# Sliding-window attention followed by spectral mixing: heads taken in pairs, deeper rings, and the on-chip accumulator banks dealt out anew

## The chip, the cores and the metric

The kernel runs on one core of a Trainium2 chip. The core has five engines that work side by side and wait for each other through semaphores: TensorE (PE in the profile, with its weight loads as PEld), VectorE (DVE), ScalarE (ACT), GpSimd (POOL) and SyncE (SP). Sixteen DMA engines move data between the main memory and the on-chip memory (SBUF). Matmul results land in a small accumulator memory (PSUM) of eight banks, from which ACT and DVE read them. The metric is the device time of one execution in microseconds (us), lower is better.

The kernel is written against a layer that takes tiles from pools, puts in every semaphore by itself, and lays out the order of each engine's instructions at compile time. A pool with `bufs=n` has n buffers for each kind of tile; a tile waits for its buffer until the last reader of the earlier tile is done. An operation written `nc.any` may be given to ACT, DVE or (a memset) POOL by that layer. So an edit in the source can move instructions that it doesn't name.

## The reference

The inputs are `q`, `k`, `v` of shape 8 x 8 x 576 x 64 (batch, heads, positions, head dimension), the mixing weights `moe_w_r` and `moe_w_i` of shape 64 x 512 x 512 (one matrix for each of 64 modes) and `moe_w_ch`, 512 x 512. All are float32, and so is the output, 8 x 576 x 512.

```python
def _attn_ref(q, k, v):
    window = 64
    scores = 1.0 / np.sqrt(D) * np.matmul(q, k.transpose(0, 1, 3, 2))
    rel = pos[:, None] - pos[None, :]
    mask = (rel >= 0) & (rel < window)
    scores = np.where(mask, scores, -1000000000.0)
    scores = scores - np.max(scores, axis=-1, keepdims=True)
    attn = np.exp(scores)
    attn = attn / (np.sum(attn, axis=-1, keepdims=True) + 1e-09)
    return np.matmul(attn, v)

def _moe_ref(x, w_r, w_i, w_ch):
    X = np.fft.rfft(x, axis=1)
    Xr, Xi = (np.real(X[:, :n_modes]), np.imag(X[:, :n_modes]))
    Yr = np.einsum('bmd,mde->bme', Xr, w_r) - np.einsum('bmd,mde->bme', Xi, w_i)
    Yi = np.einsum('bmd,mde->bme', Xr, w_i) + np.einsum('bmd,mde->bme', Xi, w_r)
    Y[:, :n_modes] = Yr + 1j * Yi
    y = np.fft.irfft(Y, n=S, axis=1)
    u = x + y
    return u + np.maximum(u @ w_ch, 0.0)
```

The second function takes the first one's output, with the heads laid side by side to 512 columns. A position attends only to itself and to the 63 positions before it.

## The kernel before

There are three stages.

**Attention and forward transform.** For each batch (8) and pair of heads (4), `build_qT` loads q and k as bf16 through POOL's queue, with two heads side by side in the 128 columns, and turns them with TensorE, so that the first head lies in partitions 0 to 63 and the second in 64 to 127. For each head, `stage_a` computes, for each block of 128 keys, the scores of those keys against up to 256 queries (a contraction over 64 rows), takes the exponential on ACT and multiplies by a 0/1 mask on DVE. `stage_b` multiplies the result with v, which carries a column of ones so that the sum of the weights comes out as column 65, and divides on DVE. After the eighth head of a batch, `dft_batch` takes the first 64 modes of the transform over the positions.

```python
    with ExitStack() as p1:
        qkraw = p1.enter_context(tc.tile_pool(name="qkraw", bufs=4))
        qtpool = p1.enter_context(tc.tile_pool(name="qtpool", bufs=3))
        vpool = p1.enter_context(tc.tile_pool(name="vpool", bufs=4))
        etpool = p1.enter_context(tc.tile_pool(name="etpool", bufs=12))
        smallpool = p1.enter_context(tc.tile_pool(name="smallpool", bufs=12))
        # ... (cut: xstg; the PSUM pools are ps_tr 2, ps_tr64 1, ps_s 2, ps_o 2, ps_d 1)

        def build_qT(src5, b, hp, name):
            # ... (cut: qT, ptr and raw are taken; two loads of 512 positions, one a head, on POOL's queue)
            for c in range(4):
                raw2 = raw[:, c, :, :].rearrange("p h d -> p (h d)")
                nc.tensor.transpose(out=ptr[:, c * 128:(c + 1) * 128], in_=raw2,
                                    identity=ident_bf[:, :])
            # ... (cut: a load of the last 64 positions into rawt, seen as raw3)
            ptr2 = ps_tr64.tile([128, 64], QT_DTYPE, name="pstr64")
            nc.tensor.transpose(out=ptr2[:, :64], in_=raw3, identity=ident_bf[:64, :64])
            nc.any.tensor_copy(out=qT[:, 512:576], in_=ptr2[:, :64])
            nc.any.tensor_copy(out=qT[:, 0:512], in_=ptr[:, 0:512])
            return qT

        def load_v(b, h):
            # ... (cut: vs, fp32, two loads on SP's queue; its column of ones by nc.any.memset)
            vt = vpool.tile([128, NKB, D + 1], ET_DTYPE, name="vt")
            nc.any.tensor_copy(out=vt[:, 0:4, :], in_=vs[:, 0:4, :])
            nc.any.tensor_copy(out=vt[0:64, 4, :], in_=vs[0:64, 4, :])
            return vt

        def stage_a(b, h, pp, qT, kT):
            ets = []
            for c in range(NKB):
                # ... (cut: nk, q0, nq: 128 x 256 three times, 128 x 192, 64 x 64)
                pss = ps_s.tile([128, ETW], FP32, name="pss")
                nc.tensor.matmul(out=pss[:nk, :nq], lhsT=kT[pp, q0:q0 + nk],
                                 rhs=qT[pp, q0:q0 + nq], start=True, stop=True)
                et = etpool.tile([128, ETW], ET_DTYPE, name="et")
                nc.scalar.activation(out=et[:nk, :nq], in_=pss[:nk, :nq],
                                     func=ACT_F.Exp, scale=EX_SCALE)
                nc.vector.tensor_tensor(out=et[:nk, :nq], in0=et[:nk, :nq],
                                        in1=m01[:nk, :nq], op=ALU.mult)
                ets.append((et, nk, nq))
            return ets

        def stage_b(b, h, ets, vt):
            for qb in range(NKB):
                # ... (cut: nq2, and the tiles of this block and of the one before)
                pso = ps_o.tile([128, D + 1], FP32, name="pso")
                nc.tensor.matmul(out=pso[:nq2, :], lhsT=et_c[:nk_c, 0:nq2],
                                 rhs=vt[:nk_c, qb, :], start=True, stop=(qb == 0))
                if qb >= 1:
                    nc.tensor.matmul(out=pso[:nq2, :], lhsT=et_p[:nk_p, 128:128 + nq2],
                                     rhs=vt[:nk_p, qb - 1, :], start=False, stop=True)
                rcp = smallpool.tile([128, 1], FP32, name="rcp")
                nc.vector.reciprocal(out=rcp[:nq2, :], in_=pso[:nq2, D:D + 1])
                nc.vector.tensor_scalar(out=x_sb[:nq2, b, qb, h * 64:h * 64 + 64],
                                        in0=pso[:nq2, 0:D], scalar1=rcp[:nq2, :],
                                        scalar2=None, op0=ALU.mult)
        # ... (cut: dft_batch: five matmuls into psX, a copy Xs, four transposes psXT, copies into XQ)
```

The loop runs head by head and keeps one head pending: `stage_a` of a head is written ahead of `stage_b` of the head before it.

**Mixing.** For each of 64 modes two weight matrices of 512 KB (as bf16 on chip) are loaded through POOL's queue into a pool of 22 buffers, which is filled while attention runs. Sixteen rows (8 batches, real and imaginary) are multiplied with them.

```python
        for m in range(NM):
            wr = wtpool.tile([128, NDCH, DM], W_DTYPE, name="wr", tag="wt")
            wi = wtpool.tile([128, NDCH, DM], W_DTYPE, name="wi", tag="wt")
            nc.gpsimd.dma_start(out=wr, in_=moe_w_r[m].rearrange("(c p) e -> p c e", p=128))
            nc.gpsimd.dma_start(out=wi, in_=moe_w_i[m].rearrange("(c p) e -> p c e", p=128))
            # ... (cut: eight matmuls into psm, a copy stg, a store into Yall)
```

**Inverse transform and channel product.** For each batch and block of positions: two matmuls into `psy`, the sum `ut` with attention's output, four transposes `psut`, four matmuls `pout` with `moe_w_ch`, and the output `ot`.

Of the kernel before, what the change touches and what calls it, by code (L numbers as in the profile page):

```python
# [10 lines left out]
FP32 = mybir.dt.float32  # L11
# [3 lines left out]
ALU = mybir.AluOpType  # L15
ACT_F = mybir.ActivationFunctionType

WINDOW = 64
# [3 lines left out]
QT_DTYPE = BF16  # L22
ET_DTYPE = BF16
Y_DTYPE = BF16
DEBUG_OUT = "full"
DEBUG_HL = (0, 1)
# [3 lines left out]
def kernel(  # L30
# [10 lines left out]
    nc = tc.nc  # L41
    B, H, S, D = q.shape
# [4 lines left out]
    EX_SCALE = 1.0 / float(np.sqrt(D))  # L47

    HP = H // 2
# [13 lines left out]
    nc.gpsimd.memset(m01f, 1.0)  # L63
    nc.gpsimd.affine_select(
        out=m01f, in_=m01f, compare_op=ALU.is_ge, fill=0.0,
        base=0, pattern=[[1, ETW]], channel_multiplier=-1,
    )
    nc.gpsimd.affine_select(
        out=m01f, in_=m01f, compare_op=ALU.is_ge, fill=0.0,
        base=WINDOW - 1, pattern=[[-1, ETW]], channel_multiplier=1,  # L70
    )
    m01 = consts.tile([128, ETW], BF16, name="m01")
    nc.vector.tensor_copy(out=m01, in_=m01f)

    MAGIC = 12582912.0
    PSAFE = 3.14159
# [78 lines left out]
    Yall = ypool.tile([NM, 2, B, DM], Y_DTYPE, name="Yall")  # L155

    with ExitStack() as p1:
        qkraw = p1.enter_context(tc.tile_pool(name="qkraw", bufs=4))
        qtpool = p1.enter_context(tc.tile_pool(name="qtpool", bufs=3))
        vpool = p1.enter_context(tc.tile_pool(name="vpool", bufs=4))  # L160
        etpool = p1.enter_context(tc.tile_pool(name="etpool", bufs=12))
        smallpool = p1.enter_context(tc.tile_pool(name="smallpool", bufs=12))
        xstg = p1.enter_context(tc.tile_pool(name="xstg", bufs=2))
        ps_tr = p1.enter_context(tc.tile_pool(name="ps_tr", bufs=2, space=bass.MemoryType.PSUM))
        ps_tr64 = p1.enter_context(tc.tile_pool(name="ps_tr64", bufs=1, space=bass.MemoryType.PSUM))
        ps_s = p1.enter_context(tc.tile_pool(name="ps_s", bufs=2, space=bass.MemoryType.PSUM))
# [28 lines left out]
        def load_v(b, h):  # L195
            vs = vpool.tile([128, NKB, D + 1], FP32, name="vs")
            nc.sync.dma_start(
                out=vs[:, 0:4, 0:D],
                in_=v[b, h, 0:512, :].rearrange("(c p) d -> p c d", p=128),
            )  # L200
            nc.sync.dma_start(out=vs[0:64, 4:5, 0:D],
                              in_=v[b, h, 512:576, :].rearrange("(c p) d -> p c d", p=64))
            nc.any.memset(vs[:, :, D:D + 1], 1.0)  # L203
            vt = vpool.tile([128, NKB, D + 1], ET_DTYPE, name="vt")
            nc.any.tensor_copy(out=vt[:, 0:4, :], in_=vs[:, 0:4, :])
            nc.any.tensor_copy(out=vt[0:64, 4, :], in_=vs[0:64, 4, :])
            return vt

        def stage_a(b, h, pp, qT, kT):
            ets = []  # L210
            for c in range(NKB):
                nk = min(128, S - c * 128)
                q0 = c * 128
                nq = min(ETW, S - q0)
                pss = ps_s.tile([128, ETW], FP32, name="pss")
                nc.tensor.matmul(out=pss[:nk, :nq],  # L216
                                 lhsT=kT[pp, q0:q0 + nk],
                                 rhs=qT[pp, q0:q0 + nq],
                                 start=True, stop=True)
                et = etpool.tile([128, ETW], ET_DTYPE, name="et")  # L220
                nc.scalar.activation(out=et[:nk, :nq], in_=pss[:nk, :nq],  # L221
                                     func=ACT_F.Exp, scale=EX_SCALE)
                nc.vector.tensor_tensor(out=et[:nk, :nq], in0=et[:nk, :nq],  # L223
                                        in1=m01[:nk, :nq], op=ALU.mult)
                ets.append((et, nk, nq))
            return ets

        def stage_b(b, h, ets, vt):
            for qb in range(NKB):
# [34 lines left out]
                nc.scalar.mul(out=XQ[:, dch, :, b], in_=psXT[:, NM:2 * NM], mul=-1.0)  # L264

        pending = None
        last_of_batch = {}
        nheads = B * H
        for x in range(nheads):
            b, h = divmod(x, H)  # L270
            hp, hl = divmod(h, 2)
            if hl == 0:
                qT = build_qT(q, b, hp, "qTt")
                kT = build_qT(k, b, hp, "kTt")
            pp = slice(hl * 64, hl * 64 + 64)
            if hl in DEBUG_HL:
                vt = load_v(b, h)
                ets = stage_a(b, h, pp, qT, kT)
            if pending is not None:
                stage_b(*pending)  # L280
                pb = pending[0]
                if pending[1] == H - 1 and DEBUG_OUT not in ("x", "qt"):
                    dft_batch(pb)
            pending = (b, h, ets, vt) if hl in DEBUG_HL else None
        if pending is not None:
            stage_b(*pending)
            if DEBUG_OUT not in ("x", "qt"):
                dft_batch(pending[0])

    if DEBUG_OUT in ("x", "qt", "xq"):  # L290
        if DEBUG_OUT == "qt":
# [100 lines left out]
```

The softmax here doesn't subtract the row's maximum and nothing guards it: scores larger than these inputs give would overflow.

## Time and profile before

| what | value |
|---|---|
| time, median of 4 runs | 685.84 us (684.93 to 686.52) |
| span of the profiled execution | 683.9 us, 8003 instructions |
| mean granted TensorE clock | 0.932 |
| PE busy | 497.4 us (73%) in 2200 matmuls |
| PEld busy | 215.9 us (32%) |
| DVE busy | 250.6 us (37%) |
| ACT busy | 246.5 us (36%) |
| POOL busy | 239.8 us (35%) |
| DMA | 98.06 MB, mean 143 GB/s |

The profile comes from the hardware profiler. A line such as `L233 PE MATMUL pso<-vt,et 128*128 128x65 bf16` gives the source line, the engine, the operation, the tile written and the tiles read, and for a matmul the rows and columns of the array in use, then the shape of what streams through. In the kernel before, L181 and L190 are the transposes in `build_qT`, L191 and L192 the copies after them, L205 and L206 the casts to `vt`, L216, L221 and L223 the score, exponential and mask of `stage_a`, L233 and L239 the two matmuls of `stage_b`, L244 and L245 its division, L253 and L260 the transform, L309 and L310 the weight loads. Matmuls overlap each other, and their ends are modelled, so the distance between two starts says more than a duration. The shares of busy time are means over the three stages; each stage has to be read by itself.

### The profile page before, as it was taken

How to read it: one execution, taken by the hardware profiler on the slowest of the kernel's cores; microseconds unless marked ns; L12 is line 12 of the kernel's file. 1: busy time of each engine (PE TensorE's matmuls, PEld its weight loads, DVE VectorE, ACT ScalarE, POOL GpSimd, SP SyncE). 2: the span in 40 equal slices, each digit the busy share in tenths (PEclk: the TensorE clock that was granted, in tenths of full speed). 3: DMA queues.
4: the chain of work that ended last, by engine and by line, in shares of the span. 5: the costliest groups of instructions: out<-in, count | busy, mean ns of one | idle time of the engine just before them, and what ended most of it. 6: DMA issues, size and time to landing. Idle time of an engine off the chain costs nothing.

```text
span 683.9 us, 8003 instructions
## 1 busy us (share of the span) xinstructions
PE 497.4 (73%) x2200; PEld 215.9 (32%) x2200; DVE 250.6 (37%) x1167; ACT 246.5 (36%) x716; POOL 239.8 (35%) x384
## 2 busy tenths in 40 slices
PE   2788998989898988788455465455455455799996
PEld 1443444444444443323111111111111111455553
DVE  5875766666666666800000000000000000456654
ACT  4856666666666666343111111111111111122221
POOL 9885766665545420032223233232232220000000
PEclk9999999999999999999888888888888888899999
DMA  9999999999767641039999999999999999122232
GB/s 117 118 120 168 153 177 157 176 164 149 71 69 72 69 55 27 0 56 209 207 207 207 207 207 207 207 207 208 207 207 207 207 207 151 63 90 103 99 109 92
DMA packets 191165, 98.06 MB, mean 143 GB/s; under 512 B 119440, under 2 KB 186000, under 8 KB 191120
## 3 DMA queue, kind: packets, MB, share of 16 engines
q0 software_dynamic: 144912, 77.62, 82.4%
q1 hardware_dynamic: 46208, 19.94, 11.7%
q8 instruction: 17, 0.28, 0.2%
q14 instruction: 28, 0.23, 0.1%
HBM read 163.58 MB, written 9.44 MB: 253 GB/s over the span
## 4 chain that ended last, share of the span: by engine, by line
DMA 40%; PE 36%; ACT 9%; issue 8%; DVE 6%; SPq 1%; ACTq 0%; POOL 0%; POOLq 0%; DVEq 0%
DMA wi<-in_moe_w_i_dram 39%; PE pss L216 8%; PE pout L352 7%; PE pstr L181 5%; PE pso L233 5%; ACT utt L349 3%; PE psut L345 3%; ACT et L221 3%; PE pso L239 2%; PE psX L253 2%; PE psXT L260 2%; DVE et L223 1%; DVE x_sb L245 1%; PE pstr L190 1%; DVE rcp L244 1%
## 5 line engine op out<-in xcount | busy, mean ns | idle before, releaser
L315 PE MATMUL psm<-wi,XQ 128*16 128x512 bf16 x256 | 120.0, 469 | 100.4 <-DMA wi<-in_moe_w_i_dram 100.3
L313 PE MATMUL psm<-wr,XQ 128*16 128x512 bf16 x256 | 119.6, 467 | 23.5 <-DMA wr<-in_moe_w_r_dram 21.1
L221 ACT ACTIVATE et<-pss 128x256 bf16<-128x256 f32 (+2 forms) x320 | 106.4, 353 | 69.7 <-PE pso L239 37.9
L342 DVE TENSOR_TENSOR ut<-x_sb,psy 128x512 f32<-128x512 bf16 (+1 forms) x40 | 27.2, 685 | 283.9 <-PE psy L336 282.6
L318 ACT CAST stg<-psm 16x512 bf16<-16x512 f32 x63 | 36.2, 575 | 244.8 <-PE psm L315 240.2
L216 PE MATMUL pss<-qT 64*128 64x256 bf16 (+2 forms) x320 | 100.3, 342 | 21.8 <-ACT et L221 17.4
L309 POOL DMA_DIRECT2D wr<-in_moe_w_r_dram x64 | 47.9, 748 | 122.5 <-PE psm L313 60.4
L245 DVE TENSOR_SCALAR x_sb<-pso,rcp 128x64 bf16<-128x64 f32 (+1 forms) x320 | 89.3, 281 | 0.8
L313 PEld LDWEIGHTS <-XQ 128*16 128x16 bf16 x256 | 24.9, 97 | 192.3 <-issue 131.9
L310 POOL DMA_DIRECT2D wi<-in_moe_w_i_dram x64 | 47.9, 749 | 96.5 <-DMA wi<-in_moe_w_i_dram 84.4
L244 DVE RECIPROCAL rcp<-pso 128x1 f32<-128x1 f32 (+1 forms) x320 | 52.6, 164 | 78.0 <-PE pso L239 57.1
L233 PE MATMUL pso<-vt,et 128*128 128x65 bf16 (+1 forms) x320 | 76.3, 244 | 5.2 <-DVE x_sb L245 3.7
L223 DVE TENSOR_TENSOR et<-et,m 128x256 bf16<-128x256 bf16 (+2 forms) x320 | 78.1, 250 | 3.7 <-ACT et L221 3.2
L239 PE MATMUL pso<-vt,et 128*128 128x65 bf16 (+1 forms) x256 | 61.4, 248 | 0.0
L233 PEld LDWEIGHTS <-et 128*128 128x128 bf16 (+1 forms) x320 | 37.5, 118 | 69.3 <-DVE x_sb L245 34.6
L181 PE MATMUL pstr<-ident_bf,raw 128*128 128x128 bf16 x256 | 48.5, 302 | 12.9 <-DVE vs L203 8.3
L175 POOL DMA_DIRECT2D raw<-in_q_dram x64 | 49.1, 773 | 19.7 <-PE pstr L190 11.5
L352 PE MATMUL pout<-wch,utt 128*128 128x512 f32 (+1 forms) x160 | 48.1, 426 | 7.0 <-ACT utt L349 6.4
L175 POOL DMA_DIRECT2D raw<-in_k_dram x64 | 49.5, 785 | 8.7 <-PE pso L233 6.7
L349 ACT CAST utt<-psut 128x512 fp32r<-128x512 f32 (+1 forms) x39 | 21.1, 542 | 76.1 <-PE psut L345 76.1
L216 PEld LDWEIGHTS <-qT 64*128 64x128 bf16 (+1 forms) x320 | 32.1, 106 | 44.2 <-issue 25.2
L359 DVE SCALAR_TENSOR_TENSOR ot<-pout,ut 128x512 f32<-128x512 f32 (+1 forms) x40 | 27.6, 690 | 38.1 <-PE pout L352 38.1
(82 smaller groups left out, 479.1 us busy)
## 6 DMA issues: line engine op xcount, KB each, us to landing
wr<-in_moe_w_r_dram POOLq DMA_DIRECT2D x64, 512.0 KB, 20.0
wi<-in_moe_w_i_dram POOLq DMA_DIRECT2D x64, 512.0 KB, 20.0
vs<-in_v_dram SPq DMA_DIRECT2D x64, 128.0 KB, 3.2
out_dram<-ot SPq DMA_DIRECT2D x32, 256.0 KB, 2.0
raw<-in_q_dram POOLq DMA_DIRECT2D x64, 64.0 KB, 3.1
raw<-in_k_dram POOLq DMA_DIRECT2D x64, 64.0 KB, 3.5
vs<-in_v_dram SPq DMA_DIRECT2D x64, 16.0 KB, 3.1
wch<-in_moe_w_ch_dram POOLq DMA_DIRECT2D x1, 1024.0 KB, 7.5
```

Of the source, the lines that this page charges most:

```text
L175: nc.gpsimd.dma_start(out=raw[:, :, hh, :], in_=src5[b, 2 * hp + hh, 0:512, :].rearrange("(c t) d -> t c d", t=128),)
L181: nc.tensor.transpose(out=ptr[:, c * 128:(c + 1) * 128], in_=raw2, identity=ident_bf[:, :])
L216: nc.tensor.matmul(out=pss[:nk, :nq], lhsT=kT[pp, q0:q0 + nk], rhs=qT[pp, q0:q0 + nq], start=True, stop=True)
L221: nc.scalar.activation(out=et[:nk, :nq], in_=pss[:nk, :nq], func=ACT_F.Exp, scale=EX_SCALE)
L223: nc.vector.tensor_tensor(out=et[:nk, :nq], in0=et[:nk, :nq], in1=m01[:nk, :nq], op=ALU.mult)
L233: nc.tensor.matmul(out=pso[:nq2, :], lhsT=et_c[:nk_c, 0:nq2], rhs=vt[:nk_c, qb, :], start=True, stop=(qb == 0))
L239: nc.tensor.matmul(out=pso[:nq2, :], lhsT=et_p[:nk_p, 128:128 + nq2], rhs=vt[:nk_p, qb - 1, :], start=False, stop=True)
L244: nc.vector.reciprocal(out=rcp[:nq2, :], in_=pso[:nq2, D:D + 1])
L245: nc.vector.tensor_scalar(out=x_sb[:nq2, b, qb, h * 64:h * 64 + 64], in0=pso[:nq2, 0:D], scalar1=rcp[:nq2, :], scalar2=None, op0=ALU.mult)
L313: nc.tensor.matmul(out=psm[:, :], lhsT=XQ[:, dch, m, B:3 * B], rhs=wr[:, dch, :], start=(dch == 0), stop=False)
L315: nc.tensor.matmul(out=psm[:, :], lhsT=XQ[:, dch, m, 0:2 * B], rhs=wi[:, dch, :], start=False, stop=(dch == NDCH - 1))
L352: nc.tensor.matmul(out=pout[:nt, :], lhsT=utt[:, ech * nt:(ech + 1) * nt], rhs=wch[:, ech, :], start=(ech == 0), stop=(ech == NDCH - 1))
```

## The change

The loop goes over pairs of heads. The scores of both heads for one block of keys are written one after the other: first the two matmuls, then the two exponentials and masks. `stage_b` follows for both heads of the pair before. With more tiles in flight, the rings of buffers grow: the `et` ring from 12 to 20, `qkraw` from 4 to 6, `vpool` from 4 to 5, the ring of `rcp` from 12 to 16. The transpose of the last 64 positions goes into the same bank as the other four, which makes one copy of 576 columns out of two (64 and 512) and frees a bank; `ps_o` gets it, 3 instead of 2. The float32 mask is built in a pool that is given back, which frees the room. It is meant to keep more independent work in flight for TensorE and to let the two heads' scores stand side by side. The mixing and the last stage are as they were.

```diff
-    m01f = consts.tile([128, ETW], FP32, name="m01f")
...  (cut: the lines that fill m01f, the same in both)
+    with tc.tile_pool(name="mask_tmp", bufs=1) as mtmp:
+        m01f = mtmp.tile([128, ETW], FP32, name="m01f")

-        qkraw = p1.enter_context(tc.tile_pool(name="qkraw", bufs=4))
+        qkraw = p1.enter_context(tc.tile_pool(name="qkraw", bufs=6))
         qtpool = p1.enter_context(tc.tile_pool(name="qtpool", bufs=3))
-        vpool = p1.enter_context(tc.tile_pool(name="vpool", bufs=4))
-        etpool = p1.enter_context(tc.tile_pool(name="etpool", bufs=12))
-        smallpool = p1.enter_context(tc.tile_pool(name="smallpool", bufs=12))
+        vpool = p1.enter_context(tc.tile_pool(name="vpool", bufs=5))
+        etpool = p1.enter_context(tc.tile_pool(name="etpool", bufs=20))
+        smallpool = p1.enter_context(tc.tile_pool(name="smallpool", bufs=16))
-        ps_tr64 = p1.enter_context(tc.tile_pool(name="ps_tr64", bufs=1, space=bass.MemoryType.PSUM))
         ps_s = p1.enter_context(tc.tile_pool(name="ps_s", bufs=2, space=bass.MemoryType.PSUM))
-        ps_o = p1.enter_context(tc.tile_pool(name="ps_o", bufs=2, space=bass.MemoryType.PSUM))
+        ps_o = p1.enter_context(tc.tile_pool(name="ps_o", bufs=3, space=bass.MemoryType.PSUM))

-            ptr = ps_tr.tile([128, 512], QT_DTYPE, name="pstr")
+            ptr = ps_tr.tile([128, S], QT_DTYPE, name="pstr")
-            ptr2 = ps_tr64.tile([128, 64], QT_DTYPE, name="pstr64")
-            nc.tensor.transpose(out=ptr2[:, :64], in_=raw3, identity=ident_bf[:64, :64])
-            nc.any.tensor_copy(out=qT[:, 512:576], in_=ptr2[:, :64])
-            nc.any.tensor_copy(out=qT[:, 0:512], in_=ptr[:, 0:512])
+            nc.tensor.transpose(out=ptr[:, 512:576], in_=raw3, identity=ident_bf[:64, :64])
+            nc.any.tensor_copy(out=qT[:, :], in_=ptr[:, :])

-        def stage_a(b, h, pp, qT, kT):
...  (cut: its body, shown above)
+        def stage_a_pair(b, hp, qT, kT):
+            ets_pair = ([], [])
             for c in range(NKB):
+                psss = []
+                for hl in range(2):
+                    pp = slice(hl * 64, hl * 64 + 64)
+                    pss = ps_s.tile([128, ETW], FP32, name="pss")
+                    nc.tensor.matmul(out=pss[:nk, :nq],
+                                     lhsT=kT[pp, q0:q0 + nk],
+                                     rhs=qT[pp, q0:q0 + nq],
+                                     start=True, stop=True)
+                    psss.append(pss)
+                for hl in range(2):
+                    et = etpool.tile([128, ETW], ET_DTYPE, name="et")
+                    nc.scalar.activation(out=et[:nk, :nq], in_=psss[hl][:nk, :nq],
+                                         func=ACT_F.Exp, scale=EX_SCALE)
+                    nc.vector.tensor_tensor(out=et[:nk, :nq], in0=et[:nk, :nq],
+                                            in1=m01[:nk, :nq], op=ALU.mult)
+                    ets_pair[hl].append((et, nk, nq))
+            return ets_pair

-        for x in range(nheads):
...  (cut: the loop over heads)
+        for b in range(B):
+            for hp in range(HP):
                 qT = build_qT(q, b, hp, "qTt")
                 kT = build_qT(k, b, hp, "kTt")
+                vts = (load_v(b, 2 * hp), load_v(b, 2 * hp + 1))
+                ets_pair = stage_a_pair(b, hp, qT, kT)
+                if pending is not None:
+                    pb, php, pets, pvts = pending
+                    for hl in range(2):
+                        stage_b(pb, 2 * php + hl, pets[hl], pvts[hl])
+                    if php == HP - 1:
+                        dft_batch(pb)
+                pending = (b, hp, ets_pair, vts)
```

After the loop, the last pair's `stage_b` and the last batch's transform follow in the same way.

More of the change, by code (lines that the diff above doesn't have):

```diff
@@ L60 @@
     nc.vector.tensor_copy(out=ident_bf, in_=ident)
-    m01f = consts.tile([128, ETW], FP32, name="m01f")
[L63 to L71, printed above, removed]
-    m01 = consts.tile([128, ETW], BF16, name="m01")
-    nc.vector.tensor_copy(out=m01, in_=m01f)
+    m01 = consts.tile([128, ETW], BF16, name="m01")
+    with tc.tile_pool(name="mask_tmp", bufs=1) as mtmp:
+        m01f = mtmp.tile([128, ETW], FP32, name="m01f")
+        nc.gpsimd.memset(m01f, 1.0)
+        nc.gpsimd.affine_select(
+            out=m01f, in_=m01f, compare_op=ALU.is_ge, fill=0.0,
+            base=0, pattern=[[1, ETW]], channel_multiplier=-1,
+        )
+        nc.gpsimd.affine_select(
+            out=m01f, in_=m01f, compare_op=ALU.is_ge, fill=0.0,
+            base=WINDOW - 1, pattern=[[-1, ETW]], channel_multiplier=1,
+        )
+        nc.vector.tensor_copy(out=m01, in_=m01f)
     MAGIC = 12582912.0
@@ L207, in load_v @@
             return vt
-        def stage_a(b, h, pp, qT, kT):
-            ets = []
+        def stage_a_pair(b, hp, qT, kT):
+            ets_pair = ([], [])
             for c in range(NKB):
@@ L214, in stage_a @@
                 nq = min(ETW, S - q0)
[L215 to L226, printed above, removed]
+                psss = []
[15 more added lines that the diff above has]
+            return ets_pair
         def stage_b(b, h, ets, vt):
@@ L266 @@
         pending = None
-        last_of_batch = {}
-        nheads = B * H
-        for x in range(nheads):
-            b, h = divmod(x, H)
-            hp, hl = divmod(h, 2)
-            if hl == 0:
+        for b in range(B):
+            for hp in range(HP):
                 qT = build_qT(q, b, hp, "qTt")
                 kT = build_qT(k, b, hp, "kTt")
[L275 to L284, printed above, removed]
+                vts = (load_v(b, 2 * hp), load_v(b, 2 * hp + 1))
[7 more added lines that the diff above has]
+                pending = (b, hp, ets_pair, vts)
         if pending is not None:
-            stage_b(*pending)
-            if DEBUG_OUT not in ("x", "qt"):
-                dft_batch(pending[0])
+            pb, php, pets, pvts = pending
+            for hl in range(2):
+                stage_b(pb, 2 * php + hl, pets[hl], pvts[hl])
+            dft_batch(pb)
     if DEBUG_OUT in ("x", "qt", "xq"):
```

## The prediction

> **What bounds the kernel now.** I read the page's slices first, to cut the run into stages, then the table by stage, then the chain of work that ended last, in order of time, then TensorE's timeline inside one stage, and the waits last.
>
> The table by stage (columns: stretch and its length, busy time and instruction count of PE, PEld, DVE, ACT, POOL, granted clock, DMA share, GB/s):
>
> ```profile
> 0.00:57.40 57.40, 37.16 (x207) 18.48 (x207) 40.03 (x193) 36.88 (x97) 49.30 (x84) 1.00 1.17 126
> 57.40:263.00 205.60, 184.41 (x966) 87.37 (x965) 134.22 (x777) 132.35 (x457) 111.71 (x194) 1.00 1.02 119
> 263.00:300.70 37.70, 29.86 (x131) 11.72 (x131) 20.29 (x116) 19.88 (x62) 0.12 (x2) 1.00 0.02 5
> 300.70:580.20 279.50, 157.23 (x498) 48.39 (x497) 0.68 (x1) 35.65 (x62) 78.70 (x106) 0.85 1.22 203
> 580.20:683.90 103.70, 88.78 (x402) 49.94 (x400) 55.36 (x81) 21.72 (x40) 0.00 (x0) 0.96 0.26 92
> ```
>
> The first three rows are attention with the forward transform, the fourth the mixing with the 128 weight tiles, the fifth the inverse transform and channel product. The change edits only the first three. In the fourth the DMA engines move a steady 203 GB/s; in the third they stand almost still (5 GB/s). All 22 weight buffers are full by then, and the next weight transfer waits for the first mixing product, as the chain shows (start, length, what):
>
> ```profile
> 194.28 0.54 PE psX L253
> ...
> 228.53 0.54 PE psX L253
> ...
> 262.78 0.54 PE psX L253
> 264.33 36.34 issue
> 300.69 0.49 POOL wr L309
> 301.45 7.78 DMA wi<-in_moe_w_i_dram
> ```
>
> The forward transform of a batch begins every 34.25 us (228.53 - 194.28). The 106 remaining weight transfers begin at 300.69, once attention is done, and everything after takes 683.9 - 300.7 = 383.2 us. So a microsecond saved in attention should come off the total one for one: no transfer hides it, because DMA is idle for some 36 us before the hand-over.
>
> Inside attention PE is busy 184.41 of 205.60 us, ACT and DVE about 65%, POOL 54%. But is PE working or waiting? Its timeline (start, length, instruction with rows*columns in use):
>
> ```profile
> 190.15 0.26 PE L233 MATMUL pso<-vt,et 64*64 64x65 bf16 x1
> 190.34 0.26 PE L239 MATMUL pso<-vt,et 128*64 128x65 bf16 x1
> 190.53 0.23 PE L233 MATMUL pso<-vt,et 128*128 128x65 bf16 x1
> ...
> 191.41 0.24 PE L233 MATMUL pso<-vt,et 128*128 128x65 bf16 x1
> 191.45 0.24 PE L239 MATMUL pso<-vt,et 128*128 128x65 bf16 x1
> ```
>
> All five have 65 columns. Between equal shapes the next starts 0.04 us later (191.41 to 191.45); where the shape changes, 0.19 us later (190.15, 190.34, 190.53). I took every start-to-start step from 60.9 to 266.8 us, six batches, 963 steps: 406 steps within one shape take 52.4 us in all (median 0.08), 557 steps between shapes take 153.4 us (median 0.25). So three quarters of attention's time passes at changes of shape. That, more than arithmetic, sets the 34.25 us.
>
> The waits name two further limits (who waited for whom, total us, times, longest):
>
> ```profile
> ACT et L221 <- PE pso L239: 37.9, 65, 1.3
> PEld L233 <- DVE x_sb L245: 34.6, 90, 0.8
> ...
> ACT et L221 <- PE pso L233: 19.6, 25, 1.2
> ...
> PE pss L216 <- ACT et L221: 17.4, 57, 1.0
> ```
>
> The second is a `pso` matmul waiting for one of two output banks. The first and third are an exponential waiting not for its own score but for a `pso` that frees its `et` buffer.
>
> **What the Trainium skill says.** "TensorEngine Tiling (Array Packing)", Key Properties: changing the tiling mode, not just the tile, drains TensorE. The trace agrees: 0.04 against 0.19 us above. "TensorE: Matmul & The Clock Gate", Part 3, The mechanism: weight loads overlap running matmuls only where the row group differs, and matmuls in different row groups run together. No run here shows it yet: consecutive scores of the kernel before use the same half and follow at 0.165 to 0.19 us. "PSUM — Partial Sum Buffer", Specifications: eight banks of 2 KiB a partition. Both kernels use all eight (2+1+2+2+1, then 2+2+3+1), so the third `pso` bank had to come from `pstr64`. "Trainium Kernel Development and Optimization", Performance Expectations: matmul busy time misleads because matmuls are pipelined; hence steps between starts, not busy time.
>
> **The change, part by part.** Where the compiler places instructions is known from the compiled order of both programs, which has no times.
>
> 1. *Heads in pairs, the tail transpose beside its four siblings.* Up to the first mixing product both orders hold 1285 matmuls; changes of tiling shape between neighbours fall from 726 to 615. What is one worth? After a short 128*128 `pso` the next `pso` comes after 0.05 us, but a score at best after 0.175; after a transpose 0.08 against 0.22 to 0.25; after a 256-wide score 0.165 to 0.19 against 0.30 to 0.32. A change costs some 0.14 us more. 111 x 0.14 = 15.5 us.
> 2. *Scores of two heads in different row halves.* 97 neighbouring score pairs of one shape now lie in different halves (58 such pairs lay in one half before). If the second starts about 0.05 us after the first, each saves 0.12: 11.6 us. With nothing here to show it, I credit half: 6 us.
> 3. *A third `pso` bank.* Steps from `pso` to `pso` average 0.087 us against 0.049 undisturbed. Over the 236 such steps of the old order that is 9 us. Between the last write to a bank and its next use lay 6 other matmuls (median in the compiled order), now 9. I take two thirds: 6 us.
> 4. *`et` from 12 to 20.* In the compiled order, 250 of 320 exponentials wait for a later `pso`, after the change 165. Two score banks remain, so a late exponential holds the next score: 17.4 us above, a third of it 5 to 6; I take 5.
> 5. *One copy of 576 instead of 64 and 512.* 64 copies of some 0.21 us vanish, about 13 us of ACT and DVE time. Of the remaining 64, ACT does 60; and it also takes 18 more of the `vt` casts from DVE (107 to 125), the long ones at 0.41. On ACT that nearly cancels. Neither engine is the bound: nothing credited.
> 6. *Deeper `qkraw`, `rcp`; temporary mask.* POOL idles 29.8 us for `rawt` buffers, but PE waited for a `raw` transfer only 3.4 us. Nothing credited.
> 7. *New costs.* ACT loads its function table nine times instead of seven, at 1.28 us each near the start: 2.6 us. The last `stage_b` now covers two heads with no score beside it: about 1.5 us. Together 4 us.
> 8. *An order laid out without this trace's times* will wait in places where the old one did not: 3 us.
>
> Sum: -15.5 - 6 - 6 - 5 + 4 + 3 = -25.5 us. 685.84 - 25.5 = 660.3, rounded to 660. As a cross-check I gave each neighbouring pair in the new order for batches 1 to 6 its mean step from the old trace: 31.9 us a batch with no credit for row halves, 30.1 with full credit. Against 34.3 that is 2.4 to 4.2 us, over eight batches 19 to 34, before the 4 us of new costs.
>
> **The rivals.** (a) *The score loop, not the shapes, paces attention.* There are still only two `pss` banks, and a pair now takes both; the next score waits for an exponential (0.38 us) whatever PE does. For it: ACT's long waits and ACT's share near 65%, which rises when the batch shortens. Against it: PE waited for `et` only 17.4 us in all. It would leave 678 to 690. (b) *Loading is the bound early on.* POOL is busy 49.3 of the first 57.4 us, and DMA's share stays near 1.3 to about 150 us. Then only later batches gain, about 10 to 13 us: 673 to 676. Against it: batches took 34.25 us both under full DMA load and after the weights had stopped, so I doubt it beyond batch 0. (c) *The rings have no slack.* Two pairs in flight hold exactly 20 `et` and 4 of 5 `vt`; an in-order ACT that waits for a `vt` release holds exponentials behind it. It would make 690 to 700. Against it: fewer exponentials wait for a release than before, and `vt` is needed a whole pair later. (d) *Full overlap of row halves and of the bank waits*: 645 to 650.
>
> **Range and chances.** The counted terms lie between 15 us (shapes alone, nothing else) and 40 us (all in full). With rival (b) at the upper end the range is 645 to 676. Two per cent faster means below 672.1: shapes alone would just reach it. I give 0.80 to faster, 0.15 to within 2%, mostly (a) and (b), and 0.05 to slower, which is (c).
>
> **What would show it.** Right: forward transforms some 31 us apart instead of 34.25; the first late weight transfer near 275 us instead of 300.69; about 383 us after it, unchanged; neighbouring scores in different halves under 0.1 us apart (step 2); the `pso` wait on `x_sb` well under 34.6 us (step 3); fewer `et` waits on `pso` (step 4). Wrong: the spacing stays at 34 although shape changes fell (rival a); it shortens only after about 200 us (b); ACT idles for `pso` or `vt` longer than before (c); or the part after the hand-over moves from 383.

## The result and the profile after

The changed kernel takes 656.26 us (median of 8 runs, 655.12 to 656.96) against 686.15 us before: a ratio of 0.9564, with a 95% interval of 0.9554 to 0.9573. The prediction was 660.0, range 645 to 676.

The changed kernel's table by stage first, its stretches cut at the same events as before: start to the first batch's transform, six batches, the last batch to the hand-over, mixing, last stage.

```profile
0.00:61.30 61.30, 37.71 (x224) 18.15 (x224) 39.77 (x185) 44.06 (x105) 54.56 (x92) 1.00 1.19 121
61.30:236.90 175.60, 165.06 (x959) 79.94 (x958) 121.21 (x746) 137.57 (x438) 105.73 (x191) 1.00 1.17 139
236.90:271.30 34.40, 28.04 (x125) 10.92 (x125) 17.22 (x108) 17.55 (x54) 0.01 (x1) 1.00 0.00 1
271.30:550.80 279.50, 165.39 (x498) 49.37 (x497) 0.68 (x1) 35.60 (x62) 78.54 (x106) 0.79 1.22 203
550.80:654.70 103.90, 88.98 (x403) 49.96 (x400) 55.34 (x81) 21.69 (x40) 0.00 (x0) 0.96 0.26 92
```

Six batches take 175.60 us instead of 205.60, and the last two stages what they took before. The hand-over to mixing moved from 300.70 to 271.30 us; from there to the end it is 383.4 us (383.2 before). The chain of work that ended last (start, length, step) shows the spacing of the transforms in the changed kernel:

```profile
120.06 0.54 PE psX L256
...
178.62 0.54 PE psX L256
...
207.89 0.54 PE psX L256
...
231.52 39.76 issue
...
272.05 9.01 DMA wi<-in_moe_w_i_dram
```

From 178.62 to 207.89 is 29.27 us a batch (34.25 before). The first batch goes the other way: its first transform starts at 59.80 us instead of 54.40. POOL's timeline (start, length, instruction, idle time before it and what ended it) says where that begins:

```profile
3.13 0.76 POOL L175 DMA_DIRECT2D raw<-in_q_dram  x1
7.33 0.41 POOL L110 IOTA Afm<- 128x320 f32 x1 [3.44 <-DVE m L74]
```

`Afm` now lies where the temporary mask lay, so POOL waits 3.44 us for the copy `m` that reads the mask. The loads that stand behind it in POOL's order are late with it: k's first one is issued at 9.43 us (5.88 before).

The waits of the changed kernel, the counterparts of those shown before:

```profile
PEld L236 <- DVE x_sb L248: 30.0, 71, 1.2
...
ACT et L224 <- PE pso L242: 24.6, 46, 0.9
...
PE pss L217 <- ACT et L224: 2.6, 9, 0.6
```

Exponentials that wait for a `pso` fell from 57.5 to 24.6 us, scores that wait for an exponential from 17.4 to 2.6. The wait for an output bank hardly moved, 34.6 to 30.0: this sign of the prediction ("well under 34.6") did not come.

### The profile page after: what moved, and what is told of

Its sections match the earlier page's. It is cut to its first block, busy times and chain, and to the rows that moved or that the text cites. A ratio compares the mean times of both kernels' runs of the same rounds, so it can differ in the third digit from the quotient of the medians.

```text
span 654.7 us, 7799 instructions
## 1 busy us (share of the span) xinstructions
PE 485.2 (74%) x2200; PEld 208.3 (32%) x2200; DVE 234.2 (36%) x1118; ACT 256.5 (39%) x699; POOL 238.8 (36%) x388
## 4 chain that ended last, share of the span: by engine, by line
DMA 43%; PE 32%; issue 9%; ACT 9%; POOL 3%; DVE 3%; SPq 0%; ACTq 0%; POOLq 0%; DVEq 0%
DMA wi<-in_moe_w_i_dram 41%; PE pout L351 7%; PE pss L217 6%; PE pso L236 4%; PE pstr L181 4%; ACT utt L348 3%; PE psut L344 3%; PE psX L256 2%; PE pso L242 2%; POOL raw L175 2%; ACT et L224 2%; ACT qT L190 2%; PE psXT L263 2%; PE pstr L189 1%; DVE et L226 1%
## 5 line engine op out<-in xcount | busy, mean ns | idle before, releaser
L314 PE MATMUL psm<-wi,XQ 128*16 128x512 bf16 x256 | 123.8, 483 | 95.8 <-DMA wi<-in_moe_w_i_dram 95.6
L312 PE MATMUL psm<-wr,XQ 128*16 128x512 bf16 x256 | 125.7, 491 | 19.8 <-DMA wr<-in_moe_w_r_dram 18.1
L224 ACT ACTIVATE et<-pss 128x256 bf16<-128x256 f32 (+2 forms) x320 | 106.5, 353 | 38.4 <-PE pso L242 24.6
L217 PE MATMUL pss<-qT 64*128 64x256 bf16 (+2 forms) x320 | 92.6, 344 | 4.7 <-ACT et L224 2.6
L312 PEld LDWEIGHTS <-XQ 128*16 128x16 bf16 x256 | 25.5, 99 | 190.5 <-issue 132.7
L236 PE MATMUL pso<-vt,et 128*128 128x65 bf16 (+1 forms) x320 | 73.7, 243 | 4.4 <-DVE x_sb L248 3.8
L248 DVE TENSOR_SCALAR x_sb<-pso,rcp 128x64 bf16<-128x64 f32 (+1 forms) x320 | 75.7, 275 | 0.1
L226 DVE TENSOR_TENSOR et<-et,m 128x256 bf16<-128x256 bf16 (+2 forms) x320 | 69.9, 253 | 1.7 <-ACT et L224 1.1
L247 DVE RECIPROCAL rcp<-pso 128x1 f32<-128x1 f32 (+1 forms) x320 | 46.6, 157 | 57.2 <-PE pso L242 52.8
L242 PE MATMUL pso<-vt,et 128*128 128x65 bf16 (+1 forms) x256 | 59.3, 248 | 0.0
L181 PE MATMUL pstr<-ident_bf,raw 128*128 128x128 bf16 x256 | 40.5, 302 | 18.3 <-DMA raw<-in_q_dram 9.0
L314 PEld LDWEIGHTS <-XQ 128*16 128x16 bf16 x256 | 27.6, 108 | 44.6 <-issue 28.6
```

Of the source, the lines that this page charges most:

```text
L224: nc.scalar.activation(out=et[:nk, :nq], in_=psss[hl][:nk, :nq], func=ACT_F.Exp, scale=EX_SCALE)
L236: nc.tensor.matmul(out=pso[:nq2, :], lhsT=et_c[:nk_c, 0:nq2], rhs=vt[:nk_c, qb, :], start=True, stop=(qb == 0))
L312: nc.tensor.matmul(out=psm[:, :], lhsT=XQ[:, dch, m, B:3 * B], rhs=wr[:, dch, :], start=(dch == 0), stop=False)
L314: nc.tensor.matmul(out=psm[:, :], lhsT=XQ[:, dch, m, 0:2 * B], rhs=wi[:, dch, :], start=False, stop=(dch == NDCH - 1))
```

## The experiments

The expectations were written before each run. "Shape changes" counts neighbouring matmuls of different tiling shape in the compiled order up to the first mixing product.

**Both heads' scores in one half.** The second head's scores repeat the first's; otherwise nothing is left out, and TensorE's order is the same.

```diff
-                    pp = slice(hl * 64, hl * 64 + 64)
+                    pp = slice(0, 64)
```

> The changed kernel, but both heads' scores are computed from partitions 0 to 63 (the second head repeats the first one's scores; nothing else is left out). The compiled order of TensorE is the same, with the same 615 changes of tiling shape; only the 97 neighbouring score pairs now lie in one half. Theory that the two halves run side by side: pairs that follow 0.003 to 0.07 us apart in the changed kernel (about half of them) go back to 0.165 to 0.19 us, in all 5 to 7 us more, so 661 to 663 us. Rival, that the two score banks pace these pairs anyway: 656 to 658 us.

Measured: 659.78 us, ratio 0.9614 (0.9595 to 0.9632). That is 3.5 us over the changed kernel, below the 5 to 7 expected and above the rival. TensorE's timeline at the same place in the third batch's transform, changed kernel first, then this one:

```profile
121.86 0.40 PE L217 MATMUL pss<-qT 64*128 64x256 bf16 x2
```

```profile
122.60 0.60 PE L217 MATMUL pss<-qT 64*128 64x256 bf16 x2
```

Two scores take 0.40 us in different halves, where one alone takes 0.39; in one half they take 0.60. In six batches of the changed kernel 17 of 72 such pairs started within 0.004 us of each other (the expectation had about half under 0.07); none of the 192-wide ones did (0.345 us at least, in either kernel). The other 55 have a common mark in the trace: the second score starts 0.05 us after the end of the exponential that read the same bank two scores before. So halves do run side by side, but most pairs wait for a score bank.

**The mask among the setup tiles.** It is taken from the pool of the other setup tiles, which is opened ahead of it for this; no setup tile lies over it then.

```diff
-    with tc.tile_pool(name="mask_tmp", bufs=1) as mtmp:
-        m01f = mtmp.tile([128, ETW], FP32, name="m01f")
+        m01f = stmp.tile([128, ETW], FP32, name="m01f")
```

> The changed kernel, with the float32 mask tile taken from the pool of the other setup tiles, so that no setup tile lies over it. Seen in the changed kernel: the first batch's transform begins 5.4 us later than before (59.8 against 54.4 us), after POOL waited 3.4 us with its iota, and with it the first loads of q and k, for the copy that reads the mask. Theory that the reuse of the mask's room costs the start: the first transform goes back to about 54.4 us and the total to 650.5 to 652 us. Rival, that the start is late because heads go in pairs and loads crowd: it stays at 59 to 60, and the total at 655 to 657 us.

Measured: 651.95 us, ratio 0.9502 (0.9482 to 0.9522). POOL's timeline in this kernel:

```profile
1.90 0.42 POOL L109 IOTA Afm<- 128x320 f32 x1
...
3.64 1.65 POOL L174 DMA_DIRECT2D raw<-in_q_dram  x2
```

The wait is gone, the first transform starts at 55.1 us, and the spacing is 29.27 us as in the changed kernel. The theory holds. The compiled order of this kernel also has seven table loads again instead of nine, so how the 4.3 us divide between the mask's wait and the loads stays open.

**Everything but the pairs, and the third bank alone.** Both are edits to the kernel before, with its loop over single heads. The bank part, which both have (the 64-row transpose goes into `ptr[:, 512:576]`):

```diff
-        ps_tr64 = p1.enter_context(tc.tile_pool(name="ps_tr64", bufs=1, space=bass.MemoryType.PSUM))
-        ps_o = p1.enter_context(tc.tile_pool(name="ps_o", bufs=2, space=bass.MemoryType.PSUM))
+        ps_o = p1.enter_context(tc.tile_pool(name="ps_o", bufs=3, space=bass.MemoryType.PSUM))
-            ptr = ps_tr.tile([128, 512], QT_DTYPE, name="pstr")
+            ptr = ps_tr.tile([128, S], QT_DTYPE, name="pstr")
-            nc.any.tensor_copy(out=qT[:, 512:576], in_=ptr2[:, :64])
-            nc.any.tensor_copy(out=qT[:, 0:512], in_=ptr[:, 0:512])
+            nc.any.tensor_copy(out=qT[:, :], in_=ptr[:, :])
```

The first of the two also has the temporary mask and the rings of the change:

```diff
-        qkraw = p1.enter_context(tc.tile_pool(name="qkraw", bufs=4))
+        qkraw = p1.enter_context(tc.tile_pool(name="qkraw", bufs=6))
-        vpool = p1.enter_context(tc.tile_pool(name="vpool", bufs=4))
-        etpool = p1.enter_context(tc.tile_pool(name="etpool", bufs=12))
-        smallpool = p1.enter_context(tc.tile_pool(name="smallpool", bufs=12))
+        vpool = p1.enter_context(tc.tile_pool(name="vpool", bufs=5))
+        etpool = p1.enter_context(tc.tile_pool(name="etpool", bufs=20))
+        smallpool = p1.enter_context(tc.tile_pool(name="smallpool", bufs=16))
```

> The kernel before with everything of the change but the pairs: deeper rings, temporary mask, one transposed bank, third output bank; the loop goes head by head. Changes of shape: 653 (before 726, changed kernel 615). Theory that shape changes at 0.14 us each are the largest term: 73 fewer give 10 us, bank and rings some 9, and the late start costs 5: about 672 us (668 to 676). Rival, that rings and bank do all of it: 655 to 660. Rival, that the pairs do all of it: 684 to 690.

> The kernel before with the transposes in one bank and the third output bank alone. Changes of shape: 737 (before 726). Theory of the prediction: 11 more changes cost 1.5 us, the third bank brings up to 6: 680 to 684 us. Rival, that the output banks are the main limit: 665 to 674 us.

Measured: 665.04 us, ratio 0.9695 (0.9674 to 0.9716), and 672.98 us, ratio 0.9809 (0.9791 to 0.9826). Both beat the theory, the first by 3 us, the second by 7 and with 11 more shape changes than before; the second one's rival holds. Here count and time part for the first time.

**One transposed bank without the third output bank.**

```diff
...  (cut: the 64-row transpose goes into `ptr`, as above)
-        ps_tr64 = p1.enter_context(tc.tile_pool(name="ps_tr64", bufs=1, space=bass.MemoryType.PSUM))
-            nc.any.tensor_copy(out=qT[:, 512:576], in_=ptr2[:, :64])
-            nc.any.tensor_copy(out=qT[:, 0:512], in_=ptr[:, 0:512])
+            nc.any.tensor_copy(out=qT[:, :], in_=ptr[:, :])
```

> The kernel before with the transposes in one bank and one copy of 576, but still two output banks (the eighth bank stays unused). Changes of shape: 692 (before 726). The kernel with the third output bank as well took 672.98 us, 13 less than before, twice what the prediction gave the third bank, with 11 more changes of shape than before. Theory that the third output bank brings nearly all of the 13: this one takes 680 to 685 us (the 34 fewer changes give at most 5). Rival, that the single transposed bank and single copy bring most of it (no wait for the one bank of the tail, 64 copies fewer): 672 to 677 us.

Measured: 687.68 us, ratio 1.002 (1.001 to 1.0031). That is above both expectations: 34 fewer shape changes gained nothing here either. The single copy brings nothing by itself; it costs 0.2%. What it is for is the bank it frees.

**The changed kernel with two output banks.**

```diff
-        ps_o = p1.enter_context(tc.tile_pool(name="ps_o", bufs=3, space=bass.MemoryType.PSUM))
+        ps_o = p1.enter_context(tc.tile_pool(name="ps_o", bufs=2, space=bass.MemoryType.PSUM))
```

> The changed kernel with two output banks instead of three; one bank stays unused. Changes of shape: 682 (changed kernel 615). Theory that the third output bank matters as much with pairs and deep rings: 9 us for 67 more changes and 6 to 10 for bank waits: 670 to 676 us. Rival, that the other parts have made the third bank needless: 656 to 662 us.

Measured: 692.82 us, ratio 1.0103 (1.0082 to 1.0124): slower than the kernel before, and 17 us above the theory. This undoes more than the whole gain. Its waits:

```profile
ACT et L224 <- PE pso L242: 50.8, 87, 1.4
...
PEld L236 <- DVE x_sb L248: 19.9, 49, 1.6
...
PE pss L217 <- ACT et L224: 16.6, 45, 1.1
...
ACT et L224 <- PE pso L236: 11.1, 22, 0.6
```

The direct wait for an output bank is shorter than in the changed kernel (19.9 against 30.0). The loss shows elsewhere: exponentials wait for outputs 61.9 (50.8 and 11.1) instead of 24.6 us, and scores for exponentials 16.6 instead of 2.6. In the compiled order, with two banks 258 of 320 exponentials wait for an output matmul that stands behind their own score, with three 165.

**The ring of weights tiles back at 12**, on the kernel with the mask among the setup tiles.

```diff
-        etpool = p1.enter_context(tc.tile_pool(name="etpool", bufs=20))
+        etpool = p1.enter_context(tc.tile_pool(name="etpool", bufs=12))
```

> The kernel with the mask among the setup tiles (651.95 us), with the ring of weights tiles (et) back at 12. Changes of shape: 729 (617); 212 of 320 exponentials wait for an output matmul behind their own score (165). Theory that counted changes of shape set the time: 112 x 0.14 = 16 us more, 665 to 670 us. Theory of the prediction for the ring alone (5 us): 655 to 658 us. Rival, that with three output banks the ring is of no account: 651 to 654 us.

Measured: 686.33 us, ratio 0.9998 (0.9987 to 1.001). All three expectations were far too low: this too undoes the whole gain. This kernel's waits (total us, count, longest):

```profile
PEld L235 <- DVE x_sb L247: 39.9, 103, 1.2
...
ACT et L223 <- PE pso L241: 32.7, 64, 1.6
...
PE pss L216 <- ACT et L223: 18.7, 55, 1.5
...
ACT et L223 <- PE pso L235: 12.6, 17, 2.4
```

In the kernel it came from, the wait for an output bank was 30.1 us, exponentials waited for outputs 24.5 (here 45.3, two lines together) and scores for exponentials 2.9. At 0.11 to 0.14 us each, the 112 more shape changes would come to 12 to 16 of the 34 us (an estimate); the rest is waits.

**The ring of raw tiles back at 4**, on the same kernel.

```diff
-        qkraw = p1.enter_context(tc.tile_pool(name="qkraw", bufs=6))
+        qkraw = p1.enter_context(tc.tile_pool(name="qkraw", bufs=4))
```

> The kernel with the mask among the setup tiles (651.95 us), with the ring of raw q and k tiles back at 4; the compiled order of TensorE has the same 617 changes of shape. Theory of the prediction, that this ring brings nothing because TensorE hardly waits for these loads: 651 to 653 us. Rival, that the faster attention stage now needs the loads earlier: 655 to 665 us.

Measured: 652.18 us, ratio 0.9497 (0.948 to 0.9515). No effect, as the prediction had it.

**The freed bank for scores, and a fourth output bank.** Both on the kernel with the mask among the setup tiles. First:

```diff
-        ps_s = p1.enter_context(tc.tile_pool(name="ps_s", bufs=2, space=bass.MemoryType.PSUM))
-        ps_o = p1.enter_context(tc.tile_pool(name="ps_o", bufs=3, space=bass.MemoryType.PSUM))
+        ps_s = p1.enter_context(tc.tile_pool(name="ps_s", bufs=3, space=bass.MemoryType.PSUM))
+        ps_o = p1.enter_context(tc.tile_pool(name="ps_o", bufs=2, space=bass.MemoryType.PSUM))
```

Second:

```diff
-        ps_tr = p1.enter_context(tc.tile_pool(name="ps_tr", bufs=2, space=bass.MemoryType.PSUM))
-        ps_o = p1.enter_context(tc.tile_pool(name="ps_o", bufs=3, space=bass.MemoryType.PSUM))
+        ps_tr = p1.enter_context(tc.tile_pool(name="ps_tr", bufs=1, space=bass.MemoryType.PSUM))
+        ps_o = p1.enter_context(tc.tile_pool(name="ps_o", bufs=4, space=bass.MemoryType.PSUM))
```

> The kernel with the mask among the setup tiles (651.95 us), with the freed bank given to the scores (3) instead of the outputs (2). Changes of shape: 602 (617 with the outputs at 3). In the changed kernel pairs of 192-wide scores follow 0.346 us apart, which is a wait for a score bank, not for the array. Theory that the score banks are now the tighter ring: 646 to 651 us. Rival, that the output banks are: 657 to 668 us.

> The kernel with the mask among the setup tiles (651.95 us), with one bank taken from the transposes (1) and given to the outputs (4). In its compiled order TensorE changes shape 701 times (617 before this edit), but only 104 of 320 exponentials wait for an output matmul behind their own score (165). Theory that counted changes of shape set the time: 84 x 0.14 = 12 us more, 662 to 666 us. Rival, that the output banks set it through these waits: 642 to 650 us. Third, that the single transposed bank becomes a wait of its own: over 666 us.

Measured: 665.37 us, ratio 0.97 (0.968 to 0.972), and 665.98 us, ratio 0.9702 (0.9688 to 0.9716). The first has fewer shape changes than the kernel it came from (602 against 617) and is 13 us slower, as its rival had it: the output ring is the tighter one. The second falls where counted shape changes put it, but that reading can't be told from the third one. By the estimate explained in the next part, transposes waited 21.4 us in six batches (10.4 in the changed kernel). That rise of 11 us is more than the 7.7 us by which all its waits together exceed the changed kernel's (41.7 against 34.0).

**The last block padded to a whole one**, so that no matmul of the weights with v uses part of the array.

```diff
+            nc.gpsimd.memset(qT[:, S:640], 0.0)
+            nc.gpsimd.memset(vt[64:128, 4, :], 0.0)
-                nk = min(128, S - c * 128)
+                nk = 128
-                nq = min(ETW, S - q0)
+                nq = min(ETW, 640 - q0)
-                nq2 = min(128, S - qb * 128)
+                nq2 = 128
```

(`qT` gets 640 columns, the division keeps its 64 rows, `xstg` goes to 1 for room.)

> The kernel with the mask among the setup tiles (651.95 us), and the last block of 64 positions padded to a whole block with zeros: q and k get 64 zero columns, v 64 zero rows, so every matmul of the weights with v uses the array as 128*128 and every score as 64*128. It adds work (two exponentials and masks a head over 64 columns and partitions more, 128 small memsets on POOL) and takes shape changes from 617 to 454. Theory that a change of shape costs some 0.14 us wherever it stands: 163 x 0.14 = 23 us, less 3 to 6 us of added work: 632 to 637 us. Rival, that the score loop, DVE or ACT now set the pace: 645 to 655 us.

Measured: 644.48 us, ratio 0.9393 (0.9366 to 0.9421). It is the fastest kernel of the study, but it falls between the two expectations: it brings 7.5 us of the theory's 15 to 20. The trace speaks for the rival's score loop: in six batches 55 of 78 neighbouring score pairs again started 0.05 us after the exponential that freed their bank, and the two scores of a pair lay 0.29 us apart on average, 0.19 in the kernel it came from.

**The padded kernel with k's copy on DVE.**

```diff
-            nc.any.tensor_copy(out=qT[:, 0:S], in_=ptr[:, :])
+            (nc.vector if name == "kTt" else nc.any).tensor_copy(out=qT[:, 0:S], in_=ptr[:, :])
```

> The padded kernel (644.48 us), with the copy of k's transposed tile always on DVE, q's copy still where the layer puts it: ACT then does 30 of the 64 copies at 0.66 us instead of 58, which takes some 18 us off it, and DVE gets about 12 us more. In the padded kernel ACT is busy 139.5 of 167.7 us in six batches and TensorE's granted clock there is 0.53. Changes of shape: 492 (454). Theory that ACT paces the padded kernel: 634 to 640 us. Rival, that the lowered TensorE clock does: 642 to 647 us. By counted changes of shape alone it would lose 5 us: 648 to 650 us.

Measured: 675.32 us, ratio 0.9838 (0.9822 to 0.9855), outside all three. Busy times by stage, six batches of the padded kernel first, then 190 us of this one's attention:

```profile
59.40:227.10 167.70, 154.47 (x953) 72.60 (x956) 122.46 (x745) 139.54 (x437) 119.58 (x291) 0.53 1.26 149
```

```profile
60.00:250.00 190.00, 152.73 (x925) 70.05 (x929) 128.06 (x734) 130.89 (x409) 121.00 (x291) 1.00 1.12 130
```

TensorE has its full clock here and ACT less to do, and yet the batch takes 32.99 us instead of 27.95. The waits inside attention (70 to 240 us; the padded kernel 70 to 230 us, below):

```profile
PEld L237 <- DVE x_sb L250: 30.3, 41, 2.0
...
PE pso L237 <- DVE x_sb L250: 17.0, 16, 1.7
```

```profile
PEld L237 <- DVE x_sb L250: 25.1, 42, 0.6
```

The longest wait grows from 0.6 to 2.0 us and comes once in every batch. DVE's timeline shows what stands ahead of the division that frees the output bank:

```profile
102.79 0.45 DVE L267 CAST XQ<-psXT 128x64 bf16<-128x64 f32 x1 [1.58 <-PE psXT L265]
102.93 1.09 DVE L227 TENSOR_TENSOR et<-et,m 128x256 bf16<-128x256 bf16 x5
103.94 0.29 DVE L249 RECIPROCAL rcp<-pso 128x1 f32<-128x1 f32 x3
```

DVE waits 1.58 us for a transposed piece of the transform, copies it and does five masks before it divides. So what came in front is a copy of the transform, not of k: the edit changed the whole order, and its time does not settle whether ACT paced the padded kernel. On the lowered clock the padded kernel's own trace says more. Steps of one kind took as long there, at 0.53, as in the kernel it came from, at 1.00: between two output matmuls on the whole array 0.049 us in both (medians), between two transposes 0.106 in both, from a 512-column transform matmul to the next output matmul 0.406 and 0.405. These steps show no cost of the lower clock; for others it is not shown.

## Why the prediction was right, step by step

To tell quicker steps from waits I took, for each kind of step between two matmuls (what goes before, what follows, shapes, widths, halves), the length that a tenth of its cases over all these traces stay under as its undisturbed length. The sum of these over six batches is the column "undisturbed"; the rest is waits. Steps next to a missing record (2.8 to 5.1 us) are counted in the first of the two. It is an estimate out of the traces: coarser kinds move single entries by up to some 10 us, the differences used below by up to 4.

| kernel | total us | shape changes | six batches us | undisturbed | waits |
|---|---|---|---|---|---|
| before | 686.2 | 726 | 205.6 | 162.6 | 43.0 |
| one copy alone | 687.7 | 692 | 204.3 | 155.5 | 48.8 |
| bank alone | 673.0 | 737 | 195.8 | 158.2 | 37.7 |
| rings and bank, no pairs | 665.0 | 653 | 184.1 | 150.6 | 33.5 |
| changed | 656.3 | 615 | 175.6 | 141.6 | 34.0 |
| changed, one half | 659.8 | 615 | 177.5 | 151.2 | 26.3 |
| changed, two output banks | 692.8 | 682 | 206.2 | 149.5 | 56.6 |
| mask moved | 652.0 | 617 | 175.6 | 141.6 | 34.0 |
| mask moved, et 12 | 686.3 | 729 | 205.6 | 151.8 | 53.6 |
| mask moved, padded | 644.5 | 454 | 167.7 | some 125 | some 42 |

**What bounds it, and the hand-over.** Right: what attention lost in time came off the total one for one. The first batch ends 3.9 us later (58.87 to 62.78 us, start of the last transform matmul), six batches save 30.1 us and the last one 3.2, together 29.4 us, by which the hand-over moved.

**Step 1, shape changes.** Right in size. Without the halves the undisturbed part falls from 162.6 to 151.2, 11.4 us, for 102 fewer changes in those batches (559 to 457): 0.11 us each, predicted 0.14. That the sums agree so closely (15.5 us over eight batches is 11.6 over six) is luck: 102 of the 111 fewer changes fell into these six batches, where 0.14 would have made 14.3. And the step took the count for a measure of the time. It isn't: the third bank alone saves 13 us with more changes, and `et` at 12 costs 34 with as many as before.

**Step 2, halves.** Mis-sized. 6 us were credited, 3.5 measured. The halves take 9.6 us off the undisturbed part (151.2 to 141.6), but waits give 7.7 back (26.3 to 34.0), because 55 of the 72 pairs still wait for one of two score banks; the sign named for this step, starts under 0.1 us apart, came for 18 of the 72.

**Steps 3 and 4, output bank and ring.** This is the term that was mis-sized most. 11 us over eight batches, 8.3 over six, were predicted; with the halves set aside, waits fell 16.7 us (43.0 to 26.3). By the same estimate the waits ahead of output matmuls fell from 10.6 to 5.2 us, near step 3's share (4.5 over six batches), and those ahead of scores from 20.8 to 5.3, four times step 4's share (3.8). (Step 3 gives 6 and 9 matmuls between two uses of a bank; the compiled orders have 5 and 8.) And the two were summed as if each stood alone. The runs show that they don't: the bank, with the single copy, brings 13 us to the kernel before and 37 to the changed one (656.26 against 692.82). Pairs with two banks, or with 12 `et` tiles, keep half or more of their quicker steps and lose as much to waits. Step 4 also put the fall from 250 to 165 waiting exponentials down to the ring; the compiled orders show that the bank does as much (258 to 207 without the ring; the ring 212 to 165 with the bank). Two limits remain. Each ring edit also changes the order of instructions (615 shape changes become 682 with two banks), so these runs show what a ring is worth in the order that comes with it, not in one fixed order. And the pairs with neither the deeper ring nor the third bank were not run.

**Steps 5 and 6, one copy and `qkraw`.** Right: nothing by themselves (687.68 and 652.18 us).

**Step 7, new costs.** The table loads were seen, the larger cost was not: the start lost 5.4 us where 2.6 were predicted, and moving the mask gave 4.3 back. The 1.5 us for a longer last `stage_b` came, and more: from the start of the last score to the last transform matmul it is 10.26 us (251.48 to 261.74) instead of 6.86 (284.27 to 291.13), with 36 output matmuls in it instead of 22. From there to the hand-over it is 9.55 us in both kernels.

**Step 8, new waits.** 3 us were set aside. In the changed kernel the waits of transposes rose from 6.4 to 10.4 us in six batches, about that much.

So the close total is in part luck. For six batches the terms come to 22.1 us (three quarters of 15.5 + 6 + 11 - 3), and 30.1 were measured, the surplus from waits. For the first and the last batch they come to a gain of 3.4 us (the other quarter, less 4 of new costs), and 0.7 were lost. An error of 8 us and one of 4 with the opposite sign leave the sum 4 us high. **Rivals:** (a) was alive in the changed kernel's halves, where a score bank held 55 of 72 pairs; (b) fell, since all of batches 1 to 6 gained, and the start was late because of the mask; (c) fell for `et` at 20, and the run at 12 shows what it would have been; (d) fell, since neither the halves nor the bank waits were fully hidden.

The Trainium skill's page "TensorE: Matmul & The Clock Gate", Part 3, The mechanism, has matmuls in different row groups run together, and the trace agrees: 256-wide scores started 0.003 us apart in different halves where a bank was free, and 0.165 us or more apart in the same half (0.185 in the run with one half). Its Part 1 (What's actually happening) ties a clock of half speed to windows in which TensorE was idle. The padded kernel's clock was 0.53 in attention while TensorE was busy 154.47 of 167.70 us; why it went down there stays open, as no run changed the clock alone.

## What to carry to other kernels

Where TensorE runs many short matmuls, read the distance between starts by shape before reading busy time: here a change of tiling shape cost 0.11 to 0.14 us, against 0.05 us between two 65-column matmuls of one shape. But here the reordering paid only with the rings behind it deep enough at the same moment: with either ring short, the whole gain was gone. So test each ring by taking it back from the finished version as well as by adding it to the old one, and count what the edit does to the compiled order before reading its time. A temporary pool that is closed early saves room and can put a wait on whatever is laid over it.

## What was not expected

Moving the small mask among the setup tiles was worth 4.3 us, a seventh of the whole change. Moving 28 copies of 0.66 us from ACT, busy 83% of the time, to DVE, busy 73%, gave an order that took 31 us more (644.48 to 675.32), with a copy of the transform ahead of divisions. And the granted TensorE clock inside one stage lay at 0.53 in one kernel and at 1.00 in its near twin, the slower of the two.
